# Streamed weight units at other points of the passes, in a memory-augmented recurrent attention kernel on one core

## The chip, the core and the metric

The kernel runs on one core of a Trainium2 chip. The metric is device time in microseconds of one launch; a time given for a kernel is the median of its runs. TensorE (PE) does the matrix products, ScalarE (ACT) and VectorE (DVE) empty the accumulators and do the element-wise work, GpSimd (POOL) and SyncE (SP) start transfers. Sixteen DMA engines move the data.

## What is computed

Two results are added to the input: an attention block that walks over 64 segments of 32 rows, each with a memory of 8 rows that comes out of the segment before it, and a dense layer with GELU. Cut to what matters:

```python
xn = _layernorm(x)                       # 2048 rows of 1024
out = x + A(xn, mem0, Wq, Wk, Wv, Wo) + B(xn, w1, b1, w2, b2)

def A(x, mem, Wq, Wk, Wv, Wo):           # 32 heads of 128
    for s in range(64):
        h = concat([mem, x[32*s:32*s+32]])          # 40 rows
        q, k, v = h @ Wq, h @ Wk, h @ Wv            # 1024 -> 32 x 128 each
        p = softmax(where(mask, q @ k.T / sqrt(128), -1e9))
        o = (p @ v) @ Wo                            # 4096 -> 1024
        mem = o[:8]                                 # into the next segment
        outs.append(o[8:])

def B(x, w1, b1, w2, b2):                # 1024 -> 3584 -> 1024
    return gelu(x @ w1 + b1) @ w2 + b2
```

The memory makes the 64 segments a chain: no segment can start before the one ahead of it has its first 8 rows. Each segment needs all four weight matrices, 8 MB each in bfloat16, which together don't fit on the chip beside the rest.

## The kernel before

The dense layer comes first, up to 401 us in the trace; then the loop over segments (L802), with the first segment from 401 to 440 us. The change touches only the loop.

**Units and passes.** The weights are cut into 64 units of 128 x 2048 (512 KB). `pass_order` (L74) lists them: half passes K0, Q0, K1, Q1, V0 and V1 of 8 units each, then 16 units of O, eight and eight. In a half pass every unit takes one product with the segment's 24 own rows and 8 memory rows (four matmuls of 128 x 512 at L831, side by side in four column groups of the array); an O unit is multiplied at L1068. 47 units stay in SBUF (resident). 17 are streamed. Of these, 15 are fetched again in every segment from copies in DRAM (tiles `Wc_K`, `Wc_Q`, `Wc_V`, `Wc_O`); two are kept in PSUM banks (`KEPT`, L116: the fourth streamed unit, in Q0, and the last streamed one of O) and copied into a slot by two DVE instructions (`copy_bits`, L274).

**Left rows and the four kinds.** Four segments make a group. Of each segment's 32 rows, 8 are left for the group: the left rows of four segments go through each weight together, once a group. So a segment has one of four kinds, `i4 = s % 4`. Kind 0 multiplies left rows in K0 and K1, kind 1 in V0, kind 2 in Q0 and V1, kind 3 in Q1 and O. Such a unit has two products (lhsT `hr_home` and `hrL`). At the end of a segment, around the step that hands over the memory (`put_mem`, L321), up to six resident units of the next segment's left pass are multiplied ahead (`lead_products`, L840), so in that pass only its other units have two products.

**Order by hand.** `PLACED` (L89) has one string of 64 characters for each kind, eight per half pass, where S is a streamed unit and a dot a resident one. The first string also says which units are streamed at all (`IS_STREAMED`, L95). `kind_order` (L99) puts the streamed and the resident units of each eight into those points, each sort in its own order.

**Slots.** Streamed units pass through 6 SBUF slots. When a streamed unit has been used, `unit_done` (L788) calls `start_stream` (L276): the next unit in the list `starts` gets this slot. SP holds the queue: each start waits there until PE has finished with the slot, and then issues one transfer of 512 KB (L285). The list goes in order of use, save that the two kept units start four later (`LATER`, L266), since a copy from PSUM is short. So the stream at place p of `starts` is issued on the release of the streamed unit used six before it. For example, the second streamed unit of Q1 is started by the first one of the same segment's K0, the second of O by the second of Q1, and that of V0 by the first of Q0.

**Attention inside the passes.** The small steps lie behind numbered units:

- `scores(0)` (L935; heads 0 to 15) behind unit `SCORES_0` of K1, with the exponentials (`exps`, L955: ACT, then two DVE minima at L968 and L969) following;
- `sums(0)` (L972) behind unit `SUMS_0` of Q1: eight small products (L977, L983), ACT Ln and two Exp (L988, L991), then DVE makes the weighted probabilities (L999, L1003);
- `scores(1)` behind unit `ATTEND` of V1, `values(0)` (L1010) behind units `VALUES_0` of V1, `sums(1)` behind unit `SUMS_1` of V1, `values(1)` behind unit `VALUES_1` of O.

Queries are turned at the end of Q0 and Q1: `turn_q` (L912) casts in two halves on ACT (L915) and transposes on DVE (L919). In a kind that has left rows in that pass, the left queries are first cast (`turn_qL`, L922, by way of L885 and L903) as soon as the last left product of the pass is made, and `q_left` (L925, L927) copies this segment's part into place. The order of a pass's left products is: those made ahead, then the others in pass order (L849 to L878).

POOL loads the rows of the next segment (L293) and writes results; it also renews the left rows (`renew_left`, L299).

Of the kernel before, what the change touches and what calls it, by code (L numbers as in the profile page):

```python
# [18 lines left out]
S = 2048  # L19
# [35 lines left out]
MEM_AT = 20  # L55
EARLY_SEGS = 7
LEAD_FIRST = 4
SCORES_0 = (6, 6, 6, 6)
SUMS_0 = (4, 4, 4, 4)
ATTEND = (0, 0, 1, 0)  # L60
VALUES_0 = ((4, 4), (4, 4), (3, 5), (4, 4))
SUMS_1 = (6, 6, 5, 7)
VALUES_1 = (5, 5, 5, 5)
LATER = 4
LAG = 3
STREAM_BUFS = 6
# [7 lines left out]
def pass_order():  # L74
# [12 lines left out]

ORDER = pass_order()
PLACED = (  # L89
    "..SS...." ".S..S..." "S....S.." "S......S" "S......." "S.S...S." "...SS..." "S....S.S",  # L90
    ".S.S...." "S....S.." ".S.S...." "....S..S" "......S." "SS...S.." "....S.S." "S....SS.",
    "..SS...." ".S..S..." "S...S..." "....S.S." "..S....." "...S.S.S" "...S..S." "S....SS.",
    "...SS..." ".S..S..." "..S..S.." ".SS....." "..S....." "S...S..S" "...S..S." "S....S.S",
)
IS_STREAMED = {unit: PLACED[0][n] == "S" for n, unit in enumerate(ORDER)}  # L95
assert all(placed.count("S") == STREAMED for placed in PLACED)
# [24 lines left out]
def kernel(  # L121
# [174 lines left out]
    def load_left_rows(g, out, eng=nc.sync):  # L296
        eng.dma_start(out=out, in_=rowsL_d[g, :, :])

    def renew_left(rows, s0, s1, eng):  # L299

        eng.tensor_copy(
            out=hL.rearrange("p k (t s) -> p k t s", s=GRP)[:, :, :, s0:s1],
            in_=rows.rearrange("p (k s t) -> p k t s", k=KT, s=GRP)[:, :, :, s0:s1],
        )
# [431 lines left out]
    with tc.tile_pool(name="late", bufs=1) as late:  # L736
# [9 lines left out]
        def new_acc():  # L746
            bank = free_banks.popleft()
            ps = banks.tile([P, 512], F32, name="acc", tag=bank)
            bank_of[id(ps)] = bank, ps
            return ps  # L750
# [51 lines left out]
        for s in range(NSEG):  # L802
# [46 lines left out]
            def half_pass(w, u, left, at, left_done=None):  # L849


                ps = new_acc()
                now = [i for w_, i, u_ in units[:48] if (w_, u_) == (w, u)]
                psL, ahead, order = None, [], now
                if left and led and led["next"][:2] == (w, u):
                    psL, ahead, order = led["next"][2:]
                    assert led["made"] == len(ahead)
                    led.clear()
                elif left:
                    psL = new_acc()  # L860
                lag = LAG if first else 0
                tiles = {}
                for n in range(KT + lag):
                    if n < KT:
                        tiles[now[n]] = unit_tile((w, now[n], u))
                        product(w, now[n], tiles[now[n]], hT, ps, now)
                    if n < lag:
                        continue
                    i = now[n - lag]
                    t = tiles.pop(i)  # L870
                    if left and i not in ahead:
                        product(w, i, t, hL, psL, order, True)
                    if first and (w, i, u) == IN_PSUM:
                        for b in range(2):
                            keep(IN_PSUM, 1024 * b, t[:, 1024 * b:1024 * b + 1024], b)
                    unit_done((w, i, u))
                    if left and left_done and i == order[-1]:
                        left_done(psL)  # L878
                    for fn in at.get(n - lag, ()):
                        fn()  # L880
                return ps, psL
# [43 lines left out]
            def q_left(u):  # L925

                nc.vector.tensor_copy(  # L927
                    out=q_home[:, :, 0:NL], in_=qL[u].rearrange("p h (t s) -> p h t s", s=GRP)[:, :, :, i4]
                )
# [5 lines left out]
            def scores(u):  # L935

                kT, qL_ends = st["kT", u], ends(q_home)
                sA = mixed[:, 0:160].rearrange("p (c q) -> p c q", q=40)
                sB = mixed[:, 160:224].rearrange("p (c a q) -> p c a q", a=2, q=NL)
                keys = ko_flat[u].rearrange("p (j n s) -> p j n s", j=4, s=GRP)  # L940
                for c in range(4):
                    for j in range(4):
                        q = slice(32 * j, 32 * j + 32)
                        nc.tensor.matmul(  # L944
                            sA[q, c, :], lhsT=kT[:, 4 * j + c, :], rhs=q_home[:, 4 * j + c, :],
                            start=(c == 0), stop=True, skip_group_check=True, tile_position=(0, 32 * j),
                        )
                for j in range(4):
                    q = slice(32 * j, 32 * j + 32)
                    nc.tensor.matmul(  # L950
                        sB[q, :, :, :], lhsT=keys[:, j, :, i4], rhs=qL_ends[:, 4 * j:4 * j + 4, :, :],
                        start=False, stop=True, skip_group_check=True, tile_position=(0, 32 * j),
                    )
# [56 lines left out]
            def values(u, rs):  # L1010

                V, (pdA, pdB) = st["V", u], st["pd", u]
                av = {r: new_acc() for r in rs}
                oV = {r: av[r][:, 0:320].rearrange("p (c b q) -> p c b q", c=4, b=2) for r in rs}
                for c in range(4):
                    for r in rs:
                        q = slice(64 * r, 64 * r + 64)
                        nc.tensor.matmul(  # L1018
                            oV[r][:, c, :, :], lhsT=V[q, c * P:(c + 1) * P], rhs=pdA[q, c, :, :],
                            start=(c == 0), stop=False, skip_group_check=True, tile_position=(64 * r, 0),  # L1020
                        )
                for r in rs:
                    q = slice(64 * r, 64 * r + 64)
                    nc.tensor.matmul(  # L1024
                        av[r][:, 0:320].rearrange("p (n e q) -> p n e q", n=8, q=NL)[:, :, ::4, :],
                        lhsT=VL[u][q, i4 * P:(i4 + 1) * P], rhs=pdB[q, :].rearrange("p (n a q) -> p n a q", n=8, q=NL),
                        start=False, stop=True, skip_group_check=True, tile_position=(64 * r, 0),
                    )
                for r in rs:
                    cp = nc.vector.tensor_copy if r else nc.scalar.copy  # L1030
                    h = slice(8 * r, 8 * r + 8)
                    parts = [
                        (ko[u].rearrange("p h (t s) -> p h t s", s=GRP)[:, h, :, i4], 0, NL),
                        ((outM if u else nat_home)[:, h, :], NL, 40),
                    ]
                    for out, q0, q1 in parts:
                        cp(out=out.rearrange("p (b c) q -> p c b q", b=2), in_=oV[r][:, :, :, q0:q1])  # L1037
                    let_go(av[r])
# [67 lines left out]
            if i4 == 2 and more:  # L1106
                renew_left(left_rows_in, 2, 3, mover)
            psK1, psK1L = half_pass("K", 1, left_k[1], {SCORES_0[i4]: [lambda: scores(0)]})
            if i4 == 0 and not first and more:
# [6 lines left out]
            }  # L1116
            at[4 if first else SUMS_0[i4]] = [lambda: sums(0)] + ([] if left_q[1] else [lambda: q_left(1)])
            if left_k[1]:
# [28 lines left out]
            else:  # L1147
                at.setdefault(n0, []).append(lambda: values(0, (0,)))
                at.setdefault(n1, []).append(lambda: values(0, (1,)))
            at.setdefault(5 if first else SUMS_1[i4], []).append(lambda: sums(1))  # L1150

# [9 lines left out]
            if i4 == 3 and g + 2 < NGRP:  # L1161
                load_left_rows(g + 2, left_rows_in[:, :])
            at = {VALUES_1[i4]: [lambda: values(1, (0, 1))]}
            psX = new_acc()
# [111 lines left out]
```

## Time and profile before

| what | value |
|---|---|
| median of 3 runs | 1772.6 us (1770.92 to 1780.19) |
| profiled execution | 1783.28 us, span of the profile 1781.5 us |
| loop over segments in the profile | 401 to 1775 us |
| 13 groups of four segments, 593.6 to 1692.7 us | 1099.1 us |
| PE, DVE, ACT, POOL busy | 95%, 57%, 39%, 16% of the span |
| read from HBM, written | 571.50 MB, 26.74 MB: 336 GB/s over the span |
| granted TensorE clock | 0.996 of full speed |

The profile is of one execution. "Busy" for PE is from modelled ends of pipelined matmuls, so it is not the share of its peak. The view of stages gives, for a stretch of time, each engine's busy time, the granted clock, the share of time that the 16 DMA engines had packets under way (packets can overlap, so a little over 1 is possible) and the rate. The view of waits says which engine stood idle for what: microseconds in total, how often, the longest. The chain follows the work that ended last back in time: at each step to what released it.

### The profile page before, as it was taken

The numbers are of one execution on the slowest core, as the hardware profiler recorded it, in microseconds if no ns is written. First come the engines' busy times: TensorE is split into PE (matmuls) and PEld (weight loads), VectorE is DVE, ScalarE is ACT, GpSimd is POOL, SyncE is SP. The second block draws the span as 40 slices with busy tenths as digits, with TensorE's granted clock in tenths as the row PEclk, the third lists the DMA queues.
The fourth block names the chain that finished last, engine by engine and source line by source line (L and its number), as shares of the span: only waits on it lengthen the run. The fifth ranks groups of instructions, "written<-read, shape, count | busy, mean of one in ns | idle before, by whom it ended". The sixth has DMA issues, their size and how long they took to land.

```text
span 1781.5 us, 65947 instructions
## 1 busy us (share of the span) xinstructions
PE 1694.8 (95%) x28354; PEld 838.9 (47%) x28374; DVE 1019.5 (57%) x2592; ACT 696.5 (39%) x1743; POOL 287.2 (16%) x575
## 2 busy tenths in 40 slices
PE   9999999998998999999999999999999999999998
PEld 5444444444444444444444444444444444444444
DVE  7657483825555565655655555555565656565564
ACT  6334251602333444433344333443333444343333
POOL 0000002403120211111211111121111121111120
PEclk9999999999999999999999999999999999999999
DMA  9455312779999999999999999999999999999997
GB/s 283 141 171 167 98 36 66 272 270 322 387 379 364 384 387 383 399 377 395 384 384 387 376 378 384 394 369 388 382 400 377 398 378 393 387 401 372 393 385 295
DMA packets 232072, 591.85 MB, mean 332 GB/s; under 512 B 57523, under 2 KB 88051, under 8 KB 231780
## 3 DMA queue, kind: packets, MB, share of 16 engines
q1 hardware_dynamic: 199680, 568.05, 84.7%
q0 software_dynamic: 15680, 14.35, 2.5%
q10 hardware_dynamic: 16420, 5.25, 1.2%
q8 instruction: 222, 3.64, 0.8%
q14 instruction: 70, 0.57, 0.1%
HBM read 571.50 MB, written 26.74 MB: 336 GB/s over the span
## 4 chain that ended last, share of the span: by engine, by line
PE 41%; DMA 20%; DVE 5%; ACT 3%; issue 1%; DVEq 0%; SPq 0%; ACTq 0%
PE acc L831 27%; PE acc L1068 11%; DMA u<-Wc_O 8%; DMA u<-Wc_Q 5%; DMA u<-Wc_V 3%; DMA u<-Wc_K 2%; PE acc L1018 1%; DVE kq L919 1%; DMA hr_home<-res_d 1%; ACT mixed L991 1%; ACT qL L885 1%; PE mixed L944 1%; DVE pd_main L999 1%; PE mixed L328 1%; PE acc L1024 0%
## 5 line engine op out<-in xcount | busy, mean ns | idle before, releaser
L831 PE MATMUL acc<-u,hr_home 128*32 128x512 bf16 x11520 | 758.1, 381 | 37.1 <-DMA u<-Wc_V 19.7
L831 PEld LDWEIGHTS <-hr_home 128*32 128x32 bf16 x12288 | 333.0, 97 | 336.7 <-issue 58.4
L831 PE MATMUL acc<-u,hrL 128*32 128x512 bf16 x3008 | 258.8, 381 | 0.5 <-issue 0.5
L532 PE MATMUL ps<-u 128*128 128x512 bf16 (+1 forms) x992 | 195.0, 359 | 0.0
L885 ACT CAST d_oL<-acc 128x512 bf16<-128x512 f32 x143 | 83.0, 583 | 245.0 <-PE acc L831 226.5
L274 DVE TENSOR_SCALAR u<-kept 128x512 uint32<-128x512 uint32 x254 | 162.2, 679 | 27.8 <-PE acc L831 24.3
L1068 PE MATMUL acc<-u,d_oL 128*32 128x512 bf16 x2560 | 164.8, 382 | 6.8 <-DMA u<-Wc_O 5.8
L662 PE MATMUL ps<-u 128*128 128x512 bf16 x657 | 145.2, 379 | 0.8
L1068 PE MATMUL acc<-u,kq 128*32 128x256 bf16 (+1 forms) x2688 | 133.3, 321 | 10.6 <-DMA u<-Wc_O 7.7
L532 PEld LDWEIGHTS <-u 128*128 128x128 bf16 x992 | 91.6, 98 | 101.6
L999 DVE TENSOR_TENSOR pd_main<-kq,mixed 128x320 bf16<-128x320 bf16 x128 | 62.5, 488 | 126.9 <-ACT mixed L991 126.9
L1068 PEld LDWEIGHTS <-kq 128*32 128x32 bf16 x3328 | 87.5, 97 | 87.4 <-ACT kq L1037 26.7
L915 ACT CAST kq<-acc 128x256 bf16<-128x256 f32 x256 | 89.3, 375 | 96.4 <-PE acc L831 56.6
L1238 POOL DMA_DIRECT2D out_dram<-hr_home x168 | 85.0, 513 | 250.3 <-DVE hr_home L1208 250.1
L968 DVE TENSOR_TENSOR kq<-kq,mixed 128x96 bf16<-128x96 bf16 x128 | 26.2, 205 | 169.2 <-ACT kq L961 91.2
L919 DVE STREAM_TRANSPOSE kq<-kq 128x256 bf16<-128x256 bf16 x256 | 98.1, 421 | 28.0 <-ACT kq L915 28.0
L831 PEld LDWEIGHTS <-hrL 128*32 128x32 bf16 x3200 | 84.8, 97 | 54.9 <-issue 4.9
L889 ACT CAST kq<-acc 128x512 bf16<-128x512 f32 x128 | 75.2, 587 | 74.4 <-PE mixed L950 72.0
L662 PEld LDWEIGHTS <-u 128*128 128x128 bf16 x672 | 65.6, 98 | 78.7 <-DVE u L619 0.4
L611 ACT ACTIVATE u<-ps,b1col 128x512 bf16<-128x512 f32 x112 | 76.5, 684 | 65.4 <-PE ps L532 62.5
L991 ACT ACTIVATE mixed<-mixed,small_consts 128x160 f32<-128x160 f32 x256 | 94.2, 368 | 8.4
L1068 PEld LDWEIGHTS <-d_oL 128*32 128x32 bf16 x2560 | 62.9, 97 | 62.3 <-issue 12.3
(137 smaller groups left out, 1851.4 us busy)
## 6 DMA issues: line engine op xcount, KB each, us to landing
u<-Wc_K SPq DMA_DIRECT2D x256, 512.0 KB
u<-Wc_V SPq DMA_DIRECT2D x256, 512.0 KB
u<-Wc_O SPq DMA_DIRECT2D x256, 512.0 KB
u<-Wc_Q SPq DMA_DIRECT2D x192, 512.0 KB
u<-in_B_w_dram SPq DMA_DIRECT2D x28, 512.0 KB
u<-in_A_Wq_dram SPq DMA_DIRECT2D x13, 512.0 KB
u<-in_A_Wv_dram SPq DMA_DIRECT2D x12, 512.0 KB
u<-in_A_Wk_dram SPq DMA_DIRECT2D x9, 512.0 KB
```

The source lines that it names most:

```text
L274: nc.vector.tensor_single_scalar(out=out, in_=in_, scalar=0, op=ALU.bitwise_or)
L532: nc.tensor.matmul(ps[:, SEG * s0:SEG * s1].rearrange("p (s t) -> p s t", t=SEG), lhsT=w1_sb[fb // 2][:, kt, (fb % 2) * P:(fb % 2 + 1) * P ...
L611: nc.scalar.activation(out=xb[:, :], in_=ps[:, :], func=ACT.Identity, bias=b1col[:, fb:fb + 1], scale=1.0)
L662: nc.tensor.matmul(ps[:, :], lhsT=gts[fc // 4][:, fc % 4, t * P:(t + 1) * P], rhs=w2_sb[fc // 2][:, fc % 2, cs], start=(fc == 0), stop=(fc ...
L831: nc.tensor.matmul(o, lhsT=lhs[:, i, :], rhs=m, start=(i == seq[0]), stop=(i == seq[-1]), tile_position=(0, 32 * j),)
L885: cp(out=out, in_=ps.rearrange("p (h e) -> p h e", e=32))
L915: nc.scalar.copy(out=q_home[:, h0:h1, NL:40], in_=ps[:, 32 * h0:32 * h1].rearrange("p (h e) -> p h e", e=32))
L919: nc.vector.transpose(out=half, in_=half)
L991: nc.scalar.activation(out=mixed[:, 160 * b:160 * b + 160], in_=mixed[:, 0:160], func=ACT.Exp, scale=-1.0, bias=off[:, b:b + 1],)
L999: nc.vector.tensor_tensor(out=pdA.rearrange("p c b q -> p b c q"), in0=prA[:, None, :, :].to_broadcast([P, 2, 4, 40]), in1=dd, op=ALU.mult,)
L1068: nc.tensor.matmul(acc[r0:r0 + rows, 0:256 * len(blocks)], lhsT=lhsT, skip_group_check=True, rhs=o_columns(t, k, blocks), start=start, sto ...
L1238: loads.dma_start(out=out_flat[rows, 256 * j:256 * j + 256], in_=res[32 * j:32 * j + NX, :])
```

## The change

The strings of `PLACED` change in all four kinds, and four numbers of the schedule. The number of streamed units in each group of eight stays as it is in every kind and pass.

```diff
-SCORES_0 = (6, 6, 6, 6)
-SUMS_0 = (4, 4, 4, 4)
+SCORES_0 = (6, 6, 7, 6)
+SUMS_0 = (4, 4, 4, 2)
 ATTEND = (0, 0, 1, 0)
 VALUES_0 = ((4, 4), (4, 4), (3, 5), (4, 4))
-SUMS_1 = (6, 6, 5, 7)
-VALUES_1 = (5, 5, 5, 5)
+SUMS_1 = (6, 6, 5, 6)
+VALUES_1 = (5, 5, 5, 4)
...
 PLACED = (
-    "..SS...." ".S..S..." "S....S.." "S......S" "S......." "S.S...S." "...SS..." "S....S.S",
-    ".S.S...." "S....S.." ".S.S...." "....S..S" "......S." "SS...S.." "....S.S." "S....SS.",
-    "..SS...." ".S..S..." "S...S..." "....S.S." "..S....." "...S.S.S" "...S..S." "S....SS.",
-    "...SS..." ".S..S..." "..S..S.." ".SS....." "..S....." "S...S..S" "...S..S." "S....S.S",
+    "S..S...." "S...S..." "S...S..." "S....S.." "S......." "SS....S." "....SS.." "S....S.S",
+    ".S.S...." "S....S.." ".S...S.." "...S...S" "......S." "SS...S.." "....S.S." "S....SS.",
+    "..SS...." ".S.S...." "S....S.." "....S..S" ".......S" ".S...S.S" "...S..S." "S....SS.",
+    "...SS..." ".S..S..." "..S..S.." "..S....S" ".....S.." ".S..S..S" "...S..S." ".S...S.S",
 )
```

A row is a kind (0 to 3); its eight pieces are K0, Q0, K1, Q1, V0, V1 and the two halves of O. Since the first row also chooses the streamed units, in K0, Q0, K1, Q1, V1 and the first half of O other units are streamed and others stay resident; the two kept units are the same as before.

## The prediction

> **What bounds the kernel now.** The page comes first. The chain that ended last is TensorE (PE) 41% and DMA 20%: work and transfers take turns.
>
> ```profile
> span 1781.5 us, 65947 instructions
> ...
> PE 41%; DMA 20%; DVE 5%; ACT 3%; issue 1%; DVEq 0%; SPq 0%; ACTq 0%
> ```
>
> The view of stages cuts the loop. Row one is 13 groups of four segments, 1099.1 / 13 = 84.5 us each. Then come the four kinds (0 to 3) of a group close to that mean (84.25 us), and six early microseconds of its kind 0.
>
> ```profile
> core 0: us, PE busy (x) PEld busy (x) DVE busy (x) ACT busy (x) POOL busy (x), PEclk, DMA share, GB/s
> 593.60:1692.70 1099.10, 1045.05 (x21351) 527.10 (x21350) 622.73 (x1600) 438.31 (x1209) 199.63 (x390) 1.00 1.01 386
> 1355.58:1376.75 21.17, 19.95 (x419) 9.80 (x419) 12.13 (x32) 8.77 (x24) 4.73 (x9) 1.00 0.97 357
> 1376.75:1396.74 19.99, 18.59 (x388) 9.32 (x387) 11.62 (x31) 7.70 (x22) 3.13 (x6) 1.00 1.02 400
> 1396.74:1417.23 20.49, 20.14 (x418) 10.52 (x418) 12.77 (x33) 8.76 (x24) 3.49 (x7) 1.00 1.02 397
> 1417.23:1439.83 22.60, 21.54 (x436) 10.68 (x436) 11.40 (x30) 8.51 (x23) 4.02 (x8) 1.00 1.01 392
> 1356.58:1362.58 6.00, 6.00 (x132) 3.03 (x124) 3.38 (x7) 1.82 (x4) 2.91 (x6) 1.00 0.91 300
> ```
>
> The granted clock is full, so nothing here is a clock effect. In kinds 1 to 3 the DMA engines never rest (share 1.01 to 1.02, about 396 GB/s); early in kind 0 they do: 300 GB/s for 6 us, while PE has no idle time at all. I read that as six full buffers that wait for PE to use them. So a group holds two regimes: transfers set the pace from late kind 0 on, PE sets it from the middle of kind 3 to early kind 0.
>
> The waits of PE in the same 13 groups name the stalls:
>
> ```profile
> PE acc L1068 <- DMA u<-Wc_O: 10.9, 24, 1.0
> PE acc L831 <- DMA u<-Wc_V: 10.9, 20, 2.2
> PE acc L831 <- DMA u<-Wc_Q: 9.3, 15, 1.3
> PE acc L1018 <- DVE pd_main L999: 3.2, 13, 0.3
> ```
>
> Where they lie shows in the chain of this group (start, length, what):
>
> ```profile
> 1365.10 6.54 DMA u<-Wc_O
> ...
> 1374.90 6.45 DMA u<-Wc_K
> ...
> 1386.38 6.77 DMA u<-Wc_O
> ...
> 1400.20 0.59 ACT qL L885
> ...
> 1418.32 6.07 DMA u<-Wc_Q
> ```
>
> Four transfers stand in it, each 6.1 to 6.8 us from issue to the product that waits: the second streamed unit of kind 0's O pass, of kind 1's K1, the third of kind 1's O, and the second of kind 3's Q1. Between them, in kind 2, stands the left query of Q0 on its way to scores(0).
>
> **The change, part by part.** The ruler is the time that a stream is given. Six slots go round: a stream starts when the use six before it in the starting order is done, with kept units four later. PE work between that use and the stream's own use is its margin. A product (four matmuls) takes 0.22 us, a unit with left rows two of them:
>
> ```profile
> 1423.26 0.40 PE L831 MATMUL acc<-u,hrL 128*32 128x512 bf16 x4
> 1424.43 0.40 PE L831 MATMUL acc<-u,hr_home 128*32 128x512 bf16 x4 [0.77 <-DMA u<-Wc_Q]
> 1424.64 0.40 PE L831 MATMUL acc<-u,hrL 128*32 128x512 bf16 x4
> 1424.86 0.62 PE L831 MATMUL acc<-u,hr_home 128*32 128x512 bf16 x8
> 1425.29 0.26 PE L977 MATMUL mixed<-kq,small_consts 128*32 128x160 bf16 x4
> 1425.36 0.22 PE L983 MATMUL mixed<-kq,small_consts 128*32 128x64 bf16 x4
> 1425.39 1.48 PE L831 MATMUL acc<-u,hr_home 128*32 128x512 bf16 x24
> ```
>
> *Kind 3, Q1 (positions 1 and 2 become 2 and 7).* The second stream starts when K0's first streamed unit (position 3) is done. Its margin is 4 + 8 + 8 + 2 units and one left product, 23 x 0.22 = 5.0 us; after, 28 products, 6.1 us: 1.1 us more. In this group PE lost 1424.43 - 1423.26 - 0.22 = 0.95 us, less than 1.1. On average the Wc_Q row gives 9.3 / 15 = 0.62 us idle a time, about once a group, and 0.18 us more because an unhindered product starts 0.22 us behind one that lasts 0.40: **0.80 us** a group, which I take as gone. Next late is V0's stream, whose margin grows too (2 becomes 5).
>
> *Kind 0, O pass (3, 4 become 4, 5; Q1's second from 7 to 5).* This stream starts on Q1's second release: 8 + 8 + 4 = 20 units become 2 + 8 + 8 + 5 = 23, 0.65 us more. The Wc_O row gives 10.9 / 24 + 0.18 = 0.63 us. That stall hides something: values(1) behind O unit 5 needs pd_main, and from the sums to the end of L999 is 1425.29 to 1427.29, 2.0 us, while V1's last unit and six O units are 1.5 us. Kind 1, which has no stall there, pays it as the L1018 row (once a group, 3.2 / 13 + 0.18 = 0.43 us). So kind 0 gains 0.63 - 0.43 = **0.20 us**.
>
> *Kind 2, scores(0) from unit 6 to 7, kept Q0 unit from 4 to 3.* Left query and scores lie on the chain (the cast at 1400.20 and what follows). The later unit gives 0.22 us, the earlier left product 0.22: up to 0.4 us. But kind 2 lies where the transfers set the pace, its V0 stream moves from 2 to 7 (25 to 30 products) and V1's first from 3 to 1, to 30 products or 6.5 us, near the 6.1 to 6.8 that hops take. I take 0, with -0.4 and +0.4 as ends. The kept unit has 8 products, 1.7 us, for two DVE copies; cost 0, at most 0.22 if the copy is late:
>
> ```profile
> L274 DVE TENSOR_SCALAR u<-kept 128x512 uint32<-128x512 uint32 x254 | 162.2, 679 | 27.8 <-PE acc L831 24.3 <-DMA u<-Wc_K 1.9 <-PE acc L1068 0.8
> ```
>
> *Kind 3, left query at Q1's end.* DVE's rows after the waiting product (the cast ahead of the first takes the 0.59 us of the chain's row at 1400.20):
>
> ```profile
> 1425.71 0.71 DVE L903 STREAM_TRANSPOSE qL<-qL 128x512 bf16<-128x512 bf16 x1 [1.45 <-ACT qL L885]
> 1426.80 0.49 DVE L999 TENSOR_TENSOR pd_main<-kq,mixed 128x320 bf16<-128x320 bf16 x1 [0.38 <-ACT mixed L991]
> 1427.20 0.45 DVE L1003 TENSOR_TENSOR d_oL<-kq,mixed 128x128 bf16<-128x128 bf16 x1
> 1427.69 0.23 DVE L927 COPY kq<-qL 128x128 bf16<-128x128 bf16 x1
> 1427.83 0.76 DVE L919 STREAM_TRANSPOSE kq<-kq 128x256 bf16<-128x256 bf16 x2
> ```
>
> The left rows of Q1 now end with position 7, so the cast (ACT L885), its transpose (DVE L903) and the copy (DVE L927) come behind V0's start T instead of inside Q1; turn_q's casts queue behind them on ACT, its transposes (L919) on DVE, and PE's scores(1) wait for those. SUMS_0 from 4 to 2 pays for part of it: sums start at T - 1.4 (their own 0.1, units 3 to 7 and one left product), and L1003 ends 2.36 us later (1425.29 to 1427.65), T + 1.0. The cast follows the last left product as it does now (1424.64 to 1425.71 with its own 0.59), T + 0.2 to T + 0.85; L903, behind L1003 on DVE, lasts to T + 1.7, L927 to T + 1.95, L919 to T + 2.7. Now T is 1425.39 + 3 x 0.22 = 1426.04 and L919 ends 1428.59, T + 2.55. So **+0.16 us**. Ends: 0, and 0.59 + 0.71 + 0.23 = 1.53 if all three line up behind today's chain. Sums at unit 2 themselves need the two DVE minima; I find them done 1.09 us after scores start, and PE has five products and the scores, 1.2 us:
>
> ```profile
> 1084.27 0.28 PE L944 MATMUL mixed<-kq,d_oL 128*32 128x40 bf16 x16
> ...
> 1085.18 0.18 DVE L969 TENSOR_TENSOR kq<-kq,mixed 128x64 bf16<-128x64 bf16 x1
> ```
>
> Cover 0.1 us; without it the difference.
>
> *The rest.* SUMS_1 of kind 3 at 6 is where kinds 0 and 1 have it: 0, at most 0.22. VALUES_1 at 4 leaves eleven products, 2.4 us, for the 2.0 us chain: 0, at most 0.43. Kind 1's K1 (3 to 5) gets 0.43 us more margin for the 6.45 us hop, but V1 and O behind it keep theirs, and they wait too (the Wc_V row): 0, at best -0.2. Kind 0's earlier units (K0 2 to 0, Q0 1 to 0, K1 5 to 4, V1 2 to 1) release slots 0.2 to 0.4 us earlier in the stretch where DMA rests; I count nothing of my own for that, since it is what lets the 0.80 through. The remaining moves take margin from streams that keep at least 6.5 us. Bytes, packets and SP's issues (15 streams a segment) are the same; other units become resident, as many in each pass.
>
> Sum: -0.80 - 0.20 + 0.16 = -0.84 us a group; kind 3 comes 16 times and kind 0, behind the first segment, 15 times, so 15.5 groups: **-13.0 us**. The profiled execution took 1783.28 us (span 1781.5), 0.6% above the median of the runs, 1772.6; it would be 1770.3, and the median 1759.6.
>
> Does the DMA side let it through? By the stage rows, kinds 1 to 3 move 8.0 + 8.1 + 8.9 = 25.0 MB in 63.1 us, 396 GB/s; kind 0's 357 x 21.17 = 7.6 MB would need 19.1 us at that rate: 2.1 us a group are to be had, more than 0.84.
>
> The Trainium skill speaks against any gain: Perfetto Trace Analysis, section What "DMA-bound" means, says that where the 16 engines bind, large descriptors are what matters. This change has none, so by that rule the time stays (rival B). Against that, the Trainium skill's Perfetto Trace Analysis, section Roofline, puts a lone core's 16 engines near 435 GB/s; an estimate from it is that the 32.6 MB of a group (386 GB/s x 84.5 us) need 75 us, not 82. The trace agrees with the first rule (share 1.01 at 386 GB/s), and the stages above show no more than 400.
>
> **The rivals.** *B, the wall.* The stalls only move: share 1.02 in kinds 1 to 3 speaks for it, kind 0's 300 GB/s against. Gain 0 to 0.4 us a group, so 1766 to 1773; likeliest 1771.
>
> *C, the left query.* The ACT and DVE work behind kind 3's Q1 lines up serially. It stands in the PE-paced stretch, so it adds directly. It decides once it exceeds the 0.80 + 0.20 saved; at 1.53 it is +0.53 us net, and +1.53 if the savings fall to the wall too. Middle +1.0 x 15.5: 1788. For it: today's chain runs through exactly these rows. Against: L903 needs only the cast, and L1003 is done by then.
>
> **How the numbers follow.** Within 0.5% (1763.7 to 1781.5) is about what a measurement of this kernel can't tell from no change. The forecast has 0.64, its own range -0.4 to -1.5 us a group (with kind 2's 0.4 and kind 1's 0.2), 1749 to 1766: 0.57 faster, 0.07 same. B has 0.20, all same. C has 0.16: 0.03 same, 0.13 slower. The range takes in the forecast and B and C's near edge: 1749 to 1777.
>
> **What would show it.** Right: the Wc_Q wait in kind 3's Q1 gone and kind 3 near 21.8 us; L1018 waits for L999 twice a group; kind 0's first 8 us above 300 GB/s and the loop near 390. Wrong: kinds 1 and 2 longer by what kind 3 loses (B), or PE idle ahead of scores(1) in kind 3 over 0.5 us longer (C), or sums at Q1's unit 2 waiting for DVE.

## The result, and the profile after

The changed kernel takes 1755.8 us (median of 5 runs, 1753.2 to 1757.1) where the kernel before takes 1772.6. The ratio is 0.9898, 95% interval 0.9874 to 0.9922: 14 to 22 us faster, against a forecast of 13.0 (1759.6, range 1749 to 1777), which lies just outside this interval. In the first table below the last column is the ratio less 1, times 1772.6 us.

The profiled execution of the changed kernel has a span of 1754.2 us, the one of before 1781.5. That difference of 27 us is too large: the profiled execution of before was itself 10.7 us above its median (1783.28 against 1772.6). Ratios, not spans, are used for sizes here; the profiles say where.

The view of stages, in the same order as before: 13 groups, kinds 0 to 3 of one group (82.79 us; 1078.25 / 13 = 82.94 is the mean), and six early microseconds of its kind 0.

```profile
588.19:1666.44 1078.25, 1037.51 (x21351) 527.24 (x21350) 622.40 (x1600) 436.74 (x1209) 200.48 (x390) 1.00 1.02 393
1168.64:1189.20 20.56, 19.81 (x419) 9.89 (x418) 12.30 (x33) 8.68 (x24) 4.74 (x9) 1.00 1.00 379
1189.20:1209.02 19.82, 18.29 (x386) 9.33 (x386) 11.70 (x31) 7.70 (x22) 3.15 (x6) 1.00 1.03 402
1209.02:1229.93 20.91, 20.38 (x419) 10.48 (x419) 12.77 (x33) 8.76 (x24) 3.49 (x7) 1.00 1.01 391
1229.93:1251.43 21.50, 21.25 (x436) 10.74 (x436) 11.32 (x30) 8.38 (x23) 4.03 (x8) 1.00 1.03 402
1169.64:1175.64 6.00, 6.00 (x132) 3.03 (x124) 3.38 (x7) 1.72 (x4) 3.15 (x6) 1.00 1.00 350
```

Read the last two columns against those of before. The mean rate is 393 GB/s instead of 386, and the early part of kind 0, where the DMA engines rested (share 0.91, 300 GB/s), is at share 1.00 and 350 GB/s. The bytes are the same, so the higher mean rate is the shorter time said in another way; where the engines rest less is what the early part of kind 0 shows. The group shown of before was at the low end there: over its 13 groups these 6 us hold 295 to 338 GB/s, 321 in the mean, and after the change 307 to 380, 351 in the mean. Kind 3 fell from 22.6 to 21.5 us in the groups shown, and from 22.57 to 21.86 in the mean of the 13.

What PE waits for in the 13 groups, after the change:

```profile
PE acc L831 <- DMA u<-Wc_V: 12.6, 22, 1.5
PE acc L1068 <- DMA u<-Wc_O: 6.4, 19, 0.5
PE acc L1018 <- DVE pd_main L999: 5.4, 22, 0.3
...
PE mixed L944 <- DVE kq L919: 1.5, 10, 0.2
PE acc L831 <- DMA u<-Wc_Q: 1.5, 4, 0.9
```

The wait in Q1 of kind 3 (Wc_Q, 9.3 us in 15 waits) is down to 1.5 in 4. The wait in O (Wc_O) fell from 10.9 to 6.4, and in its place values(1) waits for `pd_main` 22 times instead of 13: the chain that the transfer had hidden. The waits for Wc_V, in V0 and V1, are a little more, 12.6 for 10.9. By kind (0 to 3), PE's waits for all streams in these groups were 7.4, 14.5, 2.1 and 8.9 us before, and are 1.2, 16.9, 1.1 and 1.4 us after: those of kinds 0 and 3 are nearly gone, those of kind 1 stay.

In kind 0's O pass of the group shown, PE's rows now run without a gap through unit 5 and then wait for DVE:

```profile
1182.79 1.47 PE L1068 MATMUL acc<-u,d_oL 128*32 128x512 bf16 x24
1184.51 0.32 PE L1018 MATMUL acc<-pd_main,kq 64*128 64x80 bf16 x8 [0.25 <-DVE pd_main L999]
```

And in kind 3 both streamed units of Q1 (each followed by its left product, `hrL`) come on time. Below PE's rows are DVE's for the left query:

```profile
1235.21 1.05 PE L831 MATMUL acc<-u,hr_home 128*32 128x512 bf16 x16
1236.08 0.40 PE L831 MATMUL acc<-u,hrL 128*32 128x512 bf16 x4
1236.30 0.26 PE L977 MATMUL mixed<-kq,small_consts 128*32 128x160 bf16 x4
...
1237.47 0.40 PE L831 MATMUL acc<-u,hrL 128*32 128x512 bf16 x4
1237.69 0.62 PE L831 MATMUL acc<-u,hr_home 128*32 128x512 bf16 x8
```

```profile
1237.80 0.49 DVE L999 TENSOR_TENSOR pd_main<-kq,mixed 128x320 bf16<-128x320 bf16 x1 [0.74 <-ACT mixed L991]
1238.21 0.44 DVE L1003 TENSOR_TENSOR d_oL<-kq,mixed 128x128 bf16<-128x128 bf16 x1
1238.54 0.71 DVE L903 STREAM_TRANSPOSE qL<-qL 128x512 bf16<-128x512 bf16 x1
1239.29 0.23 DVE L927 COPY kq<-qL 128x128 bf16<-128x128 bf16 x1
1239.43 0.77 DVE L919 STREAM_TRANSPOSE kq<-kq 128x256 bf16<-128x256 bf16 x2
```

V0 starts at T = 1237.69 and L919 ends at 1240.20, T + 2.51; the prediction had T + 2.7 and before showed T + 2.55. The five DVE steps follow each other with no gap over 0.04 us. The other groups agree: in all 13, L919 ends at T + 2.50 to 2.51 here and at T + 2.55 to 2.56 in before.

### The profile page after: what moved, and what is told of

The parts are those of the page before. It is cut to its first block, busy times and chain, and to the rows that moved or that the text cites. A ratio compares the mean times of both kernels' runs of the same rounds, so it can differ in the third digit from the quotient of the medians.

```text
span 1754.2 us, 65975 instructions
## 1 busy us (share of the span) xinstructions
PE 1686.1 (96%) x28354; PEld 839.7 (48%) x28374; DVE 1019.5 (58%) x2592; ACT 694.8 (40%) x1743; POOL 288.5 (16%) x575
## 4 chain that ended last, share of the span: by engine, by line
PE 45%; DMA 16%; DVE 5%; ACT 3%; issue 1%; DVEq 0%; ACTq 0%; SPq 0%
PE acc L831 31%; PE acc L1068 10%; DMA u<-Wc_O 8%; DMA u<-Wc_Q 3%; DMA u<-Wc_V 3%; DMA hr_home<-res_d 2%; PE acc L1018 1%; ACT mixed L991 1%; DMA u<-Wc_K 1%; DVE pd_main L999 1%; DVE kq L919 1%; PE mixed L944 1%; DVE u L274 1%; PE acc L1024 1%; PE mixed L328 1%
## 5 line engine op out<-in xcount | busy, mean ns | idle before, releaser
L831 PE MATMUL acc<-u,hr_home 128*32 128x512 bf16 x11520 | 754.7, 380 | 24.4 <-DMA u<-Wc_V 15.5
L1068 PE MATMUL acc<-u,d_oL 128*32 128x512 bf16 x2560 | 162.4, 380 | 0.7 <-DMA u<-Wc_O 0.6
L1068 PE MATMUL acc<-u,kq 128*32 128x256 bf16 (+1 forms) x2688 | 134.0, 322 | 11.1 <-DMA u<-Wc_O 8.3
L999 DVE TENSOR_TENSOR pd_main<-kq,mixed 128x320 bf16<-128x320 bf16 x128 | 62.5, 488 | 125.0 <-ACT mixed L991 125.0
L1068 PEld LDWEIGHTS <-kq 128*32 128x32 bf16 x3328 | 87.2, 97 | 88.8 <-ACT kq L1037 26.4
L919 DVE STREAM_TRANSPOSE kq<-kq 128x256 bf16<-128x256 bf16 x256 | 98.2, 422 | 28.0 <-ACT kq L915 27.9
L1068 PEld LDWEIGHTS <-d_oL 128*32 128x32 bf16 x2560 | 65.4, 96 | 54.6 <-issue 2.8
```

The lines of the kernel that those rows point to most:

```text
L831: nc.tensor.matmul(o, lhsT=lhs[:, i, :], rhs=m, start=(i == seq[0]), stop=(i == seq[-1]), tile_position=(0, 32 * j),)
L919: nc.vector.transpose(out=half, in_=half)
L999: nc.vector.tensor_tensor(out=pdA.rearrange("p c b q -> p b c q"), in0=prA[:, None, :, :].to_broadcast([P, 2, 4, 40]), in1=dd, op=ALU.mult,)
L1068: nc.tensor.matmul(acc[r0:r0 + rows, 0:256 * len(blocks)], lhsT=lhsT, skip_group_check=True, rhs=o_columns(t, k, blocks), start=start, sto ...
```

## The experiments

The theory: the gain is the time that streams are given (margins), above all in kind 3's Q1, paid for in part by the chain of the left query behind it. The rivals: transfers set the pace, so stalls only move (the wall); the later left query costs more than the wait did; and, formed from the changed trace, that kind 2's scores or another first segment bring part of it.

| kernel | ratio to before | 95% interval | us |
|---|---|---|---|
| the change | 0.9898 | 0.9874 to 0.9922 | -18.1 |
| k3_q1_only | 0.9961 | 0.9945 to 0.9977 | -6.9 |
| k3_all | 0.9930 | 0.9902 to 0.9957 | -12.4 |
| k2_scores | 0.9996 | 0.9979 to 1.0013 | -0.7 |
| k2_all | 0.9993 | 0.9979 to 1.0006 | -1.2 |
| k1_row | 1.0004 | 0.9989 to 1.0018 | +0.7 |
| k0_row | 0.9981 | 0.9965 to 0.9997 | -3.4 |
| k0_k3 | 0.9905 | 0.9878 to 0.9931 | -16.8 |
| after_sums4 | 0.9930 | 0.9916 to 0.9943 | -12.4 |
| after_q1_back | 0.9986 | 0.9971 to 1.0000 | -2.5 |
| before_half | 0.9690 | 0.9661 to 0.9718 | -55.0 |
| after_half | 0.9659 | 0.9630 to 0.9687 | -60.4 |
| k2_scores_half | 0.9667 | 0.9638 to 0.9695 | -59.0 |

The traces also give the length of each kind, in us: the mean over the 13 groups of one profiled execution, from a segment's first product on its own rows behind `put_mem` to that of the next. Such a mean is good to 0.1 or 0.2 us.

| kernel | kind 0 | kind 1 | kind 2 | kind 3 |
|---|---|---|---|---|
| before | 20.96 | 20.10 | 20.92 | 22.57 |
| the change | 20.61 | 19.98 | 20.49 | 21.86 |
| k3_all | 20.81 | 20.28 | 20.67 | 21.83 |
| k0_k3 | 20.69 | 20.15 | 20.82 | 21.74 |
| k2_scores | 20.80 | 20.16 | 20.80 | 22.52 |
| k2_all | 20.88 | 19.97 | 20.55 | 22.67 |
| after_q1_back | 20.68 | 19.97 | 20.42 | 22.54 |
| before_half | 20.56 | 18.43 | 20.50 | 21.45 |
| after_half | 20.58 | 18.42 | 20.23 | 21.40 |
| k2_scores_half | 20.56 | 18.40 | 20.22 | 21.45 |

**Kind 3's Q1 alone (k3_q1_only).** Two S in one piece of the before kernel:

```diff
-    ... ".SS....." "..S....." "S...S..S" "...S..S." "S....S.S",   # kind 3, from Q1 on
+    ... "..S....S" "..S....." "S...S..S" "...S..S." "S....S.S",
```

> Before, with one edit: kind 3's streamed units of Q1 at 2 and 7 instead of 1 and 2, sums(0) left behind unit 4. Theory of margins: the wait of 0.80 us a group in Q1 goes, but the left query now stands behind late sums, so scores(1) of kind 3 moves from 2.55 to about 3.1 us behind V0's start: -0.80 + 0.55 = -0.25 us a group, 16 groups, -4 us. Wall: 0, the wait turns up at V0 or V1 of kind 3. Left query lined up serially: +0.73 us a group, +12 us.

Measured -6.9 us (-9.8 to -4.1). That excludes the wall's 0 and the serial query's +12, and lies a little beyond the -4. What paid for it shows in one row of its waits, PE waiting in scores(1) for the transposed queries; the rows are of this kernel, and of before for comparison:

```profile
PE mixed L944 <- DVE kq L919: 5.4, 21, 0.5
```

```profile
PE mixed L944 <- DVE kq L919: 2.6, 17, 0.2
```

The wait doubles and its longest is 0.5 us: with sums(0) behind unit 4, L999 and L1003 stand ahead of the left query on DVE, and L919 ends at T + 2.86 in the mean of the 13 groups (T is V0's start), where before has T + 2.55 and the expectation had 3.1. With that, -0.80 + 0.31 = -0.49 us a group makes -7.8 us, inside the interval.

**All of kind 3 (k3_all).**

```diff
-SUMS_0 = (4, 4, 4, 4)
+SUMS_0 = (4, 4, 4, 2)
-SUMS_1 = (6, 6, 5, 7)
-VALUES_1 = (5, 5, 5, 5)
+SUMS_1 = (6, 6, 5, 6)
+VALUES_1 = (5, 5, 5, 4)
...
-    "...SS..." ".S..S..." "..S..S.." ".SS....." "..S....." "S...S..S" "...S..S." "S....S.S",
+    "...SS..." ".S..S..." "..S..S.." "..S....S" ".....S.." ".S..S..S" "...S..S." ".S...S.S",
```

> Before, with the whole change of kind 3 (its row, sums(0) behind 2, sums(1) behind 6, values(1) behind 4). Theory of margins: -0.80 + 0.16 = -0.64 us a group, -10 us, most of the change's gain. Wall: between 0 and -4 us, with kinds 0 to 2 longer by what kind 3 loses.

Measured -12.4 us (-17.4 to -7.6). In its 13 groups the waits are:

```profile
PE acc L1068 <- DMA u<-Wc_O: 15.5, 31, 1.4
PE acc L831 <- DMA u<-Wc_V: 8.9, 17, 0.9
PE acc L1018 <- DVE pd_main L999: 2.9, 12, 0.3
...
PE acc L831 <- DMA u<-Wc_Q: 1.0, 2, 0.9
PE mixed L944 <- DVE kq L919: 0.9, 6, 0.2
```

Wc_Q went from 9.3 to 1.0, and Wc_O rose by 4.6 (10.9 to 15.5). That looks as if part of the stall had moved, as the wall has it, but it isn't shown: in k3_q1_only Wc_Q went as far and Wc_O is 8.3, and in the kernels that leave kinds 0 and 3 as they are (before, k1_row, k2_scores, k2_all) Wc_O is 10.9 to 13.5.

**Kind 2's scores (k2_scores, then all of kind 2, k2_all).**

```diff
-SCORES_0 = (6, 6, 6, 6)
+SCORES_0 = (6, 6, 7, 6)
...
-    "..SS...." ".S..S..." ...   # kind 2
+    "..SS...." ".S.S...." ...
```

> Before, with scores(0) of kind 2 behind unit 7 of K1 and the kept unit of Q0 at 3 instead of 4; no other streamed unit moves. The changed kernel's trace has kind 2 0.4 us shorter, where the prediction counted 0. If that is the wait of scores(0) for the left query: -0.4 us a group, -6 us, here too. If transfers set the pace in kind 2: 0, and the waits for Wc_V in V0 and V1 of kind 2 grow by as much.

Measured -0.7 us (-3.7 to +2.3): no gain that can be told, and not the 6 us. Kind 2 itself is hardly shorter (20.80 us, 20.92 before), and PE's waits for streams in it rose from 2.1 to 4.2 us in the 13 groups. The row of waits of this kernel that is largest beside O, over all kinds:

```profile
PE acc L831 <- DMA u<-Wc_Q: 12.0, 16, 1.7
```

It was 9.3 in 15, but kind 3's Q1 has little of the rise (8.4 us in 13 waits before, 9.0 in 11 here); kinds 1 and 2 have the rest. The expectation looked for the loss at V0 and V1 of kind 2: Wc_V grew there, from 0.4 to 1.4 us. So some of what the later scores give, 0.4 us in each of 13 groups, is waited for again within kind 2; where the rest went isn't shown. With the streamed units moved as well:

> Before, with the whole change of kind 2 (its row, and scores(0) behind unit 7). Scores and the kept unit alone measured no difference. If transfers set the pace there, moving V0's stream from 2 to 7 and V1's first from 3 to 1 gives at most the 0.1 us a group that V0's stream waits now: 0 to -2 us. If what the scores saved was lost only at V0's stream (unit 2), the later place lets it through: -0.4 us a group, -6 us.

Measured -1.2 us (-3.7 to +1.1). That excludes the 6 us, but not a gain of up to 3.7. Kind 2 is shorter in the traces of all four kernels that have this whole row (20.42 to 20.55 us; 20.67 to 20.92 in the other seven with whole transfers), so a small gain of kind 2's own stays possible; the run times don't show one.

**Kind 1 alone (k1_row).**

```diff
-    ".S.S...." "S....S.." ".S.S...." "....S..S" ...   # kind 1
+    ".S.S...." "S....S.." ".S...S.." "...S...S" ...
```

> Before, with kind 1's row alone (K1's second streamed unit at 5 instead of 3, Q1's first at 3 instead of 4). Theory of margins: the wait ahead of K1's second stream goes, the same time is waited at V1 and O, whose margins stay: 0 to -2 us. If every wait of PE for a stream counts by itself: -0.2 us a group, -3 us.

Measured +0.7 us (-1.9 to +3.2): no difference.

**Kind 0 alone (k0_row).**

```diff
-    "..SS...." ".S..S..." "S....S.." "S......S" "S......." "S.S...S." "...SS..." "S....S.S",
+    "S..S...." "S...S..." "S...S..." "S....S.." "S......." "SS....S." "....SS.." "S....S.S",
```

> Before, with kind 0's row alone, which also chooses other units as streamed. Theory of margins: -0.2 us in kind 0 a group, -3 us, and the wait of O's second streamed unit turns into a wait of values(1) for pd_main. If the first segment is shorter because of the other choice of units (the changed kernel's trace has it 3.3 us shorter): -3 us more, seen ahead of 440 us. Wall: 0.

Measured -3.4 us (-6.2 to -0.5), as the margins have it. The other choice of units brings no shorter first segment: with it that segment took 34.1 to 36.3 us in five profiles, without it 34.0 to 35.2 in five, and 39.2 in that of before alone. The hidden chain comes out in its waits:

```profile
PE acc L1068 <- DMA u<-Wc_O: 7.6, 20, 0.7
PE acc L1018 <- DVE pd_main L999: 5.2, 21, 0.3
```

**Kinds 0 and 3 together (k0_k3)**, both edits above in one kernel.

> Before, with the changes of kinds 0 and 3 alone (whole transfers). The prediction counts only these: what kinds 1 and 2 do is 0 by it, so this kernel should be as fast as the changed one, about -17 us against before, within 2 us. If kinds 1 and 2 add their waits once the others are relieved: 4 us or more slower than the changed one.

Measured -16.8 us (-21.6 to -12.2), 1.3 less than the whole change and inside its interval. These two rows carry most of the change, if not all; what kinds 1 and 2 add is too small for these runs to tell.

**Undoing one part of the change (after_sums4, after_q1_back).** In the changed kernel, sums(0) of kind 3 goes back behind unit 4, and in the second kernel Q1's streamed units go back too:

```diff
-SUMS_0 = (4, 4, 4, 2)
+SUMS_0 = (4, 4, 4, 4)
...
-    ... "..S....S" ".....S.." ...   # kind 3, after_q1_back only
+    ... ".SS....." ".....S.." ...
```

> The changed kernel with sums(0) of kind 3 behind unit 4 again. Theory of chains: scores(1) of kind 3 is reached 0.4 us later (L1003 ends later on DVE, and the left query's transpose stands behind it): +0.4 us a group, +6 us against the changed kernel, so about -11 us against before. If sums(0) has cover behind V0's eight units: 0, -17 us against before.

Measured -12.4 us against before (-14.9 to -10.1), 5.7 lost of the change's 18.1, as the chain has it: L919 ends at T + 2.85 in the mean instead of T + 2.51, and 0.34 us in 16 groups are 5.4. The wait for the queries is longer than in any other kernel here:

```profile
PE mixed L944 <- DVE kq L919: 7.2, 22, 0.5
```

> The changed kernel with kind 3's Q1 as before (streamed units at 1 and 2, sums(0) behind 4). Theory of margins: the 0.80 us wait is back and the left query is early again: +0.64 us a group, +10 us against the changed kernel, about -7 us against before. Wall (all parts together relieve the transfers): at most +4 us, -13 us against before.

Measured -2.5 us (-5.1 to 0): 15.6 us are lost, more than the 10 expected, and nearly all of the change. The wait in Q1 is back as it was before:

```profile
PE acc L831 <- DMA u<-Wc_V: 9.6, 17, 0.7
PE acc L831 <- DMA u<-Wc_Q: 8.6, 15, 0.9
```

What is left is about what kind 0's row brings alone (3.4). Kind 3 takes 22.54 us here and 22.57 before: without the moves in Q1, its other moves bring nothing that shows.

**Half transfers (before_half, after_half, k2_scores_half).** From the third segment on each stream fetches 1024 of its 2048 columns, and the products use these twice:

```diff
...
-            nc.sync.dma_start(out=t[:, :], in_=copies[unit])
+            w = 1024 if n >= 2 * STREAMED else 2048
+            t = t[:, 0:w]
+            nc.sync.dma_start(out=t, in_=copies[unit][:, 0:w])
...
```

> Before, with half the bytes in each streamed transfer from the third segment on: 1024 of 2048 columns are fetched, and the products read these columns twice, so part of the weights is left out while PE, ACT and DVE do as many instructions. Theory of margins: what PE waits for transfers in 13 groups (10.9 + 10.9 + 9.3 + 1.8 us idle, 71 waits with 0.18 us more each, 46 us) goes, 3.5 us a group, less what then waits on chains: 40 to 55 us below before. If PE and the chains between engines set the pace anyway: under 15 us.

Measured -55.0 us, at the far end of the 40 to 55. The stage and the only wait for a transfer in 1000 us:

```profile
600.00:1600.00 1000.00, 976.12 (x20292) 494.59 (x20296) 589.35 (x1523) 416.41 (x1148) 190.23 (x372) 1.00 0.69 209
```

```profile
PE acc L1022 <- DVE pd_main L1003: 6.3, 25, 0.3
...
PE acc L1074 <- DMA u<-Wc_O: 0.4, 1, 0.4
```

The DMA engines rest for a third of the time here, and nearly all waits that are left are for chains. (The lines have moved by a few: L1022 is L1018, L1074 is L1068.) The lengths of the kinds show what late streams cost before: 1.67 us a segment in kind 1, 1.12 in kind 3, 0.40 and 0.42 in kinds 0 and 2.

> The changed kernel with the same half transfers. If the change works through the time that streams are given, hardly anything is left of it here: of its parts only scores(0) of kind 2 (-0.4 us a group) and the later left query of kind 3 (+0.16), so 2 to 8 us below the half version of before instead of 17. If it works through shorter chains on ACT and DVE: still 12 us or more below it.

> Kind 2's scores alone, with the same half transfers. With whole transfers it gave nothing. If transfers ate it there, the wait of scores(0) is now on the path: -0.4 us a group, 6 us below the half version of before. If the moved scores save nothing at all: 0.

Medians: 1720.3 us for the half version of before, 1714.6 for that of the change, 1716.1 for kind 2's scores. So without late transfers the change is worth 5.7 us instead of 17, within the 2 to 8 expected. Kind 2's scores alone bring 4.2 there, less than the 6 expected, where they bring nothing that can be told with whole transfers. The traces put it in kind 2, which goes from 20.50 to 20.22 us, 0.28 in 16 groups or 4.5 us; the other kinds stay within 0.05.

## Why the prediction was right

- **Which regime.** That transfers set the pace in kinds 1 and 2, and PE from kind 3's Q1 to early kind 0, holds best for kind 1: half transfers shorten it by 1.67 us, and PE's waits for streams there stay (14.5 us before, 16.9 after). It is weaker for kind 2, which loses only 0.42 us to late streams. Counting kind 2's 0.4 us as nothing mattered most; taken in full it would have been 6 us more. The runs bear out a count near 0 (-0.7 and -1.2 us with whole transfers, against -4.2 with half), but leave room for up to 3.7 us.
- **Kind 3's Q1, -0.80 us a group.** It went: Wc_Q 9.3 to 1.5 us over all kinds, and in kind 3 from 13 waits of 8.4 us to 2 of 0.5.
- **Left query, +0.16.** The mechanism was right (sums(0) at 2 is what keeps it cheap, 5.7 us without), the size was not: L919 ends at T + 2.51 where T + 2.7 was forecast and T + 2.55 was there before, so -0.04 instead of +0.16. DVE's steps overlap at their ends (L903 starts at 1238.54, before L1003 is through at 1238.65, and L919 at 1239.43, before L927 is through at 1239.52), and the forecast added them up end to end. Times 16 that is 3 us; k3_all's -12.4 against -10 agrees, though its interval is too wide to show it.
- **Kind 0, -0.20.** -3.4 us measured for 15 x 0.20 = 3, with the hidden chain of values(1) as forecast (21 waits for `pd_main` instead of 13). The agreement is partly luck: the 0.63 is a mean over all 24 waits of the Wc_O row, of which 13 lie in kind 0, 7.4 us, or 0.75 us each with the 0.18; and after the change kind 0 still waits there 4 times.
- **The sum.** -13.0 forecast, -18.1 by the ratio and -16.8 by the medians. With -0.04 for the left query the sum is -1.04 x 15.5 = -16.1, inside the interval. Whether kind 2 has a part in the rest is open.
- **Rival B, the wall,** falls as a whole: kinds 0 and 3 alone bring 16.8 us where it had at most 6. It is true of kind 1. The Trainium skill's Perfetto Trace Analysis, section What "DMA-bound" means, has large descriptors as what matters where the 16 engines bind. Here the packets are the same in both kernels, and the rate went from 386 to 393 GB/s by when the transfers start: the engines were bound for most of a group, and rested in one part of it.
- **Rival C, the serial left query,** did not come about with sums(0) at 2; k3_q1_only and after_sums4 show up to 0.5 us of it a wait.

One thing stands open: why after_q1_back loses 15.6 us where k3_q1_only wins 6.9 and sums(0) 5.7 (12.6 together). The intervals of the three allow the difference; nothing here decides it.

## What to carry to other kernels

Where streams go round through a few slots, count for every stream the work between the release that starts it and its own use, and look at the smallest margins beside the time from issue to use: a stall is cheap to move where another stream has more than it needs. Before counting a saving, ask which regime its place lies in: in a stretch where transfers set the pace it can be waited for again at the next late streams (kind 2's scores: 0.7 us, within the noise, with whole transfers, 4.2 us with half). And a stall that goes can uncover a chain that it hid; its length is to be had from a place that has the chain without the stall (here kind 1).

## What the runs showed of the hardware

The first segment of the loop took 39.2 us in the profile of before, 35.8 after the change, and 34.3 in that of k1_row, which has the same first segment as before. The granted clock of TensorE differs with it:

```profile
401.24:440.40 39.16, 32.56 (x567) 15.47 (x570) 21.34 (x47) 11.12 (x27) 12.10 (x22) 0.91 0.91 323
```

```profile
400.50:434.80 34.30, 29.03 (x567) 14.29 (x569) 21.30 (x47) 11.11 (x27) 10.44 (x19) 1.00 0.98 358
```

The first row is of before (clock 0.91), the second of k1_row (1.00). So 4.9 us between these two executions lie here and are no effect of where the units stand. The clock isn't the whole of it: the first segments of k0_row and k0_k3, alike in their units, took 36.3 and 34.1 us, both at clock 1.00. What else makes it longer wasn't tried; the rates (323 against 358 GB/s) don't tell, since the bytes are nearly the same.
